# Streaming attention for one query: eight heads to a load instead of four, in three buffers, with every engine's order set by hand

## The chip, the cores and the metric

The kernel runs on one core of one Trainium2 chip. The metric is the device time of one execution in microseconds (us). A profile covers the "span" of one execution, which is about 1.7 us shorter than the reported time.

Engines: PE (TensorE, matmuls), VectorE (DVE in the profile), ScalarE (ACT), GpSimd (POOL), and the queue from which loads are issued (SP). The data come in through 16 DMA engines. The granted clock is the share of PE's full clock that the profile records; PE is called warm at full clock and cold at half.

## The reference

```python
B, H, Sq, Skv, Dh = 8, 32, 1, 4096, 128        # q, k, v in bfloat16
scale  = q.shape[-1] ** -0.5
scores = jnp.einsum('bhqd,bhkd->bhqk', q, k) * scale
attn   = softmax(scores, axis=-1)
return jnp.einsum('bhqk,bhkd->bhqd', attn, v)
```

There are 256 heads, each with one query, 4096 keys and 4096 values. K and V are 537 MB together, each byte is used once, and little is computed with it. The least that any kernel must do is bring 537 MB in.

## The kernel before

A tile holds G = 4 heads. A head lies on 32 partitions, and each partition has C = 128 of its keys (32 KiB). One load brings one tile of K or of V (4 MiB) into one of five buffers. Per tile t:

```python
G = 4; SLOTS = 5; R = 4; LAST = 8
...
def product(t, lo, hi):            # VectorE: k * q, then add the upper half of d to the lower
    for c0 in range(lo, hi, MC):   # MC = 32 keys, one chunk
        nc.vector.tensor_tensor(out=part, in0=part, in1=qb..., op=ALU.mult)
        nc.vector.tensor_tensor(out=part[:, :, 0 : D // 2], in0=..., in1=..., op=ALU.add)

def sum_over_d(t):                 # PE: 16 matmuls with the identity, sums into PSUM
    for s in range(n):
        nc.tensor.matmul(ps[:], lhsT=ident[:], rhs=kt[:, ..., s * DS : (s + 1) * DS], ...)

def weights_of(t):                 # VectorE: last sum, maximum over the head, bias
    nc.vector.tensor_reduce(out=sc[...], in_=ps[:], axis=AX.X, op=ALU.add)
    ...
    w = w_pool.tile([P, C, G], BF16, name="w", tag="w")
    for g in range(G):             # ScalarE: one exponential per head
        nc.scalar.activation(out=w[:, :, g], in_=sc[:], func=ACT.Exp, bias=bias[:, g : g + 1], ...)

def values_of(t, lo, hi):          # PE: four columns of weights at a time against V
    for c0 in range(lo, hi, CB):
        nc.tensor.matmul(avs[t][:], lhsT=w[:, c0 : c0 + CB, :], rhs=vt[:, c0 : c0 + CB, :], ...)

def norm_of(n):                    # PE: total of the weights;  VectorE: its reciprocal
    nc.tensor.matmul(zp[:], lhsT=esums..., rhs=ones[:], ...)
    nc.vector.reciprocal(out=rzs[n][:], in_=zp[:])

def result_of(t):                  # ScalarE: copy out of PSUM ("combine");  PE: pick;  ScalarE: scale, store
    ...
```

The main loop works with a lag. While tile t is multiplied, the weights of tile t-1 are made and the values of tile t-2 are summed. K is loaded two tiles ahead. The order of the main loop's instructions on each engine is left to the framework; only the end of the kernel has a set order.

```python
for t in range(NT - 1):            # NT = 64
    if t + 2 < NT: load("k", t + 2)
    load("v", t)
    ...
    product(t, 0, C // 2)
    if t > 0: weights_of(t - 1)
    product(t, C // 2, C)
    if t > 1:
        values_of(t - 2, 0, C); result_of(t - 2)
        ...
    sum_over_d(t)
```

## Time and profile before

The kernel took 1262.33 us (1262.09 to 1262.40, three runs).

| | before |
|---|---|
| loads, first packet to last | 1252.6 us |
| from the last packet to the end of the span | 6.1 us |
| rate of the slices in mid-run | 428 to 433 GB/s |
| VectorE busy, PE busy | 75 %, 67 % of the span |

The first two rows are worked out from the trace's packet records, which give start and length of every packet on the load queue (1.8 us is the start of the first one, 1254.4 us the end of the last).

From the page: the span, busy time and share of PE and VectorE, then the 40 slices of the span with DMA (tenths of the 16 engines' time) and the rate of each slice.

```profile
span 1260.5 us, 8779 instructions
...
PE 845.2 (67%) x3430; PEld 317.2 (25%) x3430; DVE 940.4 (75%) x851; ACT 164.3 (13%) x609; POOL 2.9 (0%) x14
...
DMA  9999999999999999999999999999999999999996
GB/s 400 432 431 431 430 433 430 430 430 430 432 432 430 429 433 432 432 433 431 431 432 433 428 432 432 432 429 430 432 431 430 433 432 432 430 431 431 429 424 287
```

The transfers run without a gap from the second slice to the last but one. They are the bound; the compute engines follow them.

From the timeline (start, length): PE in one tile.

```profile
648.83 9.38 PE L219 MATMUL av<-vt,w 128*16 128x512 bf16 x32 [6.55 <-DMA vt<-in_v_dram]
...
658.14 1.04 PE L167 MATMUL ps<-kt,ident 128*128 128x512 bf16 x4
...
659.42 2.77 PE L167 MATMUL ps<-kt,ident 128*128 128x512 bf16 x12
```

The 16 sum matmuls take 1.04 + 2.77 = 3.8 us.

### The profile page before, as it was taken

How to read it: one execution, taken by the hardware profiler on the slowest of the kernel's cores; microseconds unless marked ns; L12 is line 12 of the kernel's file. 1: busy time of each engine (PE TensorE's matmuls, PEld its weight loads, DVE VectorE, ACT ScalarE, POOL GpSimd, SP SyncE). 2: the span in 40 equal slices, each digit the busy share in tenths (PEclk: the TensorE clock that was granted, in tenths of full speed). 3: DMA queues.
4: the chain of work that ended last, by engine and by line, in shares of the span. 5: the costliest groups of instructions: out<-in, count | busy, mean ns of one | idle time of the engine just before them, and what ended most of it. 6: DMA issues, size and time to landing. Idle time of an engine off the chain costs nothing.

```text
span 1260.5 us, 8779 instructions
## 1 busy us (share of the span) xinstructions
PE 845.2 (67%) x3430; PEld 317.2 (25%) x3430; DVE 940.4 (75%) x851; ACT 164.3 (13%) x609; POOL 2.9 (0%) x14
## 2 busy tenths in 40 slices
PE   1666766856757667677676675766767667667578
PEld 0222222322222222222232222222222222222223
DVE  5869978687686777877778768677686777876873
ACT  0101111111101111011111110110101101111011
POOL 0000000000000000000000000000000000000000
PEclk9778878888789788887787888888888788887889
DMA  9999999999999999999999999999999999999996
GB/s 400 432 431 431 430 433 430 430 430 430 432 432 430 429 433 432 432 433 431 431 432 433 428 432 432 432 429 430 432 431 430 433 432 432 430 431 431 429 424 287
DMA packets 20569, 537.57 MB, mean 426 GB/s; under 512 B 2592, under 2 KB 2592, under 8 KB 2992
## 3 DMA queue, kind: packets, MB, share of 16 engines
q1 hardware_dynamic: 20160, 536.88, 99.2%
q8 instruction: 27, 0.44, 0.1%
q10 hardware_dynamic: 368, 0.13, 0.0%
q14 instruction: 14, 0.11, 0.0%
HBM read 536.94 MB, written 0.07 MB: 426 GB/s over the span
## 4 chain that ended last, share of the span: by engine, by line
DMA 67%; PE 24%; DVE 7%; ACT 1%; issue 0%; SPq 0%; ACTq 0%; DVEq 0%
DMA vt<-in_v_dram 66%; PE av L219 22%; DVE kt L150 4%; DVE kt L153 2%; PE ps L167 2%; DMA kt<-in_k_dram 1%; ACT w L203 0%; DVE sc L180 0%; PE op L244 0%; ACT comb L240 0%; DVE pmax L184 0%; SPq L124 0%; DVE bias L195 0%; DVE spread L186 0%; DVE nmax L191 0%
## 5 line engine op out<-in xcount | busy, mean ns | idle before, releaser
L219 PE MATMUL av<-vt,w 128*16 128x512 bf16 x2046 | 571.9, 449 | 344.1 <-DMA vt<-in_v_dram 344.1
L150 DVE TENSOR_TENSOR kt<-kt,qb 128x4096 bf16<-128x4096 bf16 x256 | 579.1, 2283 | 214.7 <-DMA kt<-in_k_dram 214.7
L219 PEld LDWEIGHTS <-w 128*16 128x16 bf16 x2046 | 207.6, 102 | 704.3 <-issue 537.3
L153 DVE TENSOR_TENSOR kt<-kt 128x2048 bf16<-128x2048 bf16 x256 | 305.7, 1215 | 0.1
L167 PE MATMUL ps<-kt,ident 128*128 128x512 bf16 x1024 | 253.2, 390 | 32.4 <-DVE kt L153 32.4
L203 ACT ACTIVATE w<-sc,bias 128x128 bf16<-128x128 f32 x256 | 110.9, 567 | 734.0 <-DVE bias L195 734.0
L167 PEld LDWEIGHTS <-ident 128*128 128x128 bf16 x1024 | 90.7, 98 | 161.3 <-issue 61.1
L203 ACT ACTIVATION_READ_ACCUMULATOR w<-sc,bias 128x1 f32 x256 | 64.8, 253 | 0.0
L180 DVE TENSOR_REDUCE sc<-ps 128x128 f32<-128x512 f32 x64 | 43.7, 683 | 24.6 <-PE ps L167 24.6
L240 ACT ACTIVATE comb<-av 16x512 bf16<-16x512 f32 x64 | 37.6, 588 | 167.8 <-PE av L219 132.2
L235 DVE RECIPROCAL rz<-zp 16x1 f32<-16x1 f32 x16 | 2.5, 155 | 66.9 <-PE zp L230 66.9
L141 ACT ACTIVATE qb<-qp 128x512 bf16<-128x512 f32 x16 | 9.6, 597 | 179.6 <-DVE kt L150 174.0
L244 PE MATMUL op<-comb,pick 16*16 16x128 bf16 x256 | 25.0, 217 | 6.4 <-ACT comb L240 6.4
L244 PEld LDWEIGHTS <-pick 16*16 16x16 bf16 x256 | 13.7, 84 | 34.2 <-issue 34.2
L135 PE MATMUL qp<-q_all,ident 16*32 16x512 bf16 x64 | 7.6, 430 | 21.6 <-ACT qb L141 14.9
L184 DVE TENSOR_REDUCE pmax<-sc 128x1 f32<-128x128 f32 x64 | 17.7, 277 | 0.1
L186 DVE TENSOR_SCALAR spread<-zero,pmax 128x32 f32<-128x32 f32 x64 | 14.9, 233 | 0.1
L195 DVE TENSOR_SCALAR bias<-own,nmax 128x4 f32<-128x4 f32 x64 | 14.3, 223 | 0.1
L191 DVE TRANSPOSE_TENSOR_REDUCE nmax<-spread 128x1 f32<-128x32 f32 x64 | 13.0, 202 | 0.1
L135 PEld LDWEIGHTS <-ident 16*32 16x32 bf16 x64 | 1.8, 89 | 28.4 <-issue 26.8
L230 PE MATMUL zp<-ones,esum 128*16 128x1 f32 x32 | 3.1, 166 | 8.1 <-ACT w L203 8.1
L259 ACT ACTIVATE stage<-op,rz 16x128 bf16<-16x128 f32 x16 | 5.7, 358 | 11.3 <-PE op L244 10.3
(21 smaller groups left out, 9.0 us busy)
## 6 DMA issues: line engine op xcount, KB each, us to landing
kt<-in_k_dram SPq DMA_DIRECT2D x63, 4096.0 KB, 35.2
vt<-in_v_dram SPq DMA_DIRECT2D x61, 4096.0 KB, 29.6
vt<-in_v_dram SPq DMA_DIRECT2D x11, 1024.0 KB, 22.3
kt<-in_k_dram SPq DMA_DIRECT2D x2, 2048.0 KB, 33.5
vt<-in_v_dram SPq DMA_DIRECT2D x1, 512.0 KB, 18.5
vt<-in_v_dram SPq DMA_DIRECT2D x2, 256.0 KB, 15.8
q_all<-in_q_dram ACTq DMA_DIRECT2D x1, 64.0 KB, 5.9
out_dram<-stage ACTq DMA_DIRECT2D x3, 16.0 KB, 9.9
```

What stands on the lines that cost most here:

```text
L150: nc.vector.tensor_tensor(out=part, in0=part, in1=qb[:, j : j + 1, :].to_broadcast([P, MC, D]), op=ALU.mult)
L153: nc.vector.tensor_tensor(out=part[:, :, 0 : D // 2], in0=part[:, :, 0 : D // 2], in1=part[:, :, D // 2 : D], op=ALU.add,)
L167: nc.tensor.matmul(ps[:], lhsT=ident[:], rhs=kt[:, u * UC : (u + 1) * UC, s * DS : (s + 1) * DS], start=(s == 0), stop=(s == n - 1),)
L180: nc.vector.tensor_reduce(out=sc[:, u * UC : (u + 1) * UC], in_=ps[:], axis=AX.X, op=ALU.add)
L184: nc.vector.tensor_reduce(out=pmax[:], in_=sc[:], axis=AX.X, op=ALU.max)
L186: nc.vector.tensor_scalar(out=spread[:], in0=zero[:], scalar1=pmax[:, 0:1], scalar2=-scale, op0=ALU.add, op1=ALU.mult,)
L191: nc.vector.tensor_reduce(out=nmax[:], in_=spread[:], axis=AX.X, op=ALU.min, apply_transpose=True)
L195: nc.vector.tensor_scalar(out=bias[:], in0=own[:], scalar1=nmax[:, 0:1], scalar2=None, op0=ALU.add)
L203: nc.scalar.activation(out=w[:, :, g], in_=sc[:], func=ACT.Exp, bias=bias[:, g : g + 1], scale=scale, accum_out=esum[:, t % R, g : g + 1],)
L219: nc.tensor.matmul(avs[t][:], lhsT=w[:, c0 : c0 + CB, :], rhs=vt[:, c0 : c0 + CB, :], start=(c0 == 0), stop=(c0 + CB == (C if t < NT - 1 e ...
L240: nc.scalar.activation(out=comb[:], in_=avs.pop(t)[:], func=ACT.Copy)
L244: nc.tensor.matmul(ops[n][:], lhsT=pick[:, m, r, :], rhs=comb[:, m * D : (m + 1) * D], start=(r == 0 and m == 0), stop=(r == R - 1 and m = ...
```

## The change

The intent is coarser work: half as many loads, each with rows twice as long, and fewer small instructions. A tile is now eight heads of 16 partitions with C = 256 keys each (64 KiB per partition, 8 MiB per load). Three such buffers fit where five of the old ones were. V follows K by one place in the queue, K is one tile ahead and not two. The values lag one tile instead of two, and the whole loop has a set order on every engine. Cut to its core:

```diff
-G = 4
-SLOTS = 5
-R = 4
+G = 8
+SLOTS = 3
+R = 2
...
     cuts = {
-        ("k", NT - 1): [C // 2] * 2,
-        ("v", NT - 3): [C // 4] * 4,
+        ("k", 0): [C // 4] * 4,
+        ("k", NT - 1): [C // 4] * 4,
         ("v", NT - 2): [C // 4] * 4,
-        ("v", NT - 1): [C // 4] * 3 + [C // 8, C // 16, LAST],
+        ("v", NT - 1): [C // 8] * 7 + [C // 16, LAST],
     }
...
-    for t in range(NT - 1):
-        if t + 2 < NT:
-            load("k", t + 2)
-        load("v", t)
-        ...
     with tc.manual_schedule():
+        q_prep(0)
+        for t in range(NT):                       # NT = 32
+            if t + 1 < NT:
+                load("k", t + 1)
+            load("v", t)
+            if t + 1 < NT:
+                q_prep(t + 1)
+            product(t, 0, UC)                     # UC = 128: four of eight chunks
+            sum_over_d(t, 0)
+            if t > 0:
+                values_of(t - 1, 0, C // 2)
+            product(t, UC, UC + MC)
+            scores_of(t, 0)
+            product(t, UC + MC, C)
+            sum_over_d(t, 1)
+            scores_of(t, 1)
+            weights_of(t)
+            if t > 0:
+                values_of(t - 1, C // 2, C)
+                if t % R == 0:
+                    norm_of(t // R - 1)
+                result_of(t - 1)
         norm_of(NQ - 1)
         values_of(NT - 1, 0, C - LAST)
         result_of(NT - 1)
```

Cut away: a small matmul that spreads the queries over 16 partitions each, a mask so that a block of 32 partitions can hold two heads, pool sizes (two buffers for w, one for sc), and LAST, the keys left for the very last matmuls, which goes from 8 to 16.

More of the change, by code (lines that the diff above doesn't have):

```diff
@@ L12 @@
 F32 = mybir.dt.float32
-G = 4
-SLOTS = 5
-R = 4
+G = 8
+SLOTS = 3
+R = 2
 OB = 4
-LAST = 8
+LAST = 16
 NEG = -1.0e30
@@ L47 @@
     NQ = NT // R
-    assert NQ <= P and C % CB == 0
-    q_n = q.rearrange("b h o d -> (b h o d)").rearrange("(n x) -> n x", n=NQ)
+    TB = 32
+    assert NH % P == 0 and P % G == 0 and TB % PH == 0 and C % CB == 0
+    q_n = q.rearrange("b h o d -> (b h o) d").rearrange("(x p) d -> p x d", p=P)
     o_n = out.rearrange("b h o d -> (b h o) d").rearrange("(n u x) d -> n x u d", u=OB, x=RG)
@@ L57 @@
     q_pool = ctx.enter_context(tc.tile_pool(name="q_pool", bufs=2))
-    w_pool = ctx.enter_context(tc.tile_pool(name="w_pool", bufs=3))
-    small = ctx.enter_context(tc.tile_pool(name="small", bufs=4))
-    o_pool = ctx.enter_context(tc.tile_pool(name="o_pool", bufs=2))
+    w_pool = ctx.enter_context(tc.tile_pool(name="w_pool", bufs=2))
+    sc_pool = ctx.enter_context(tc.tile_pool(name="sc_pool", bufs=1))
+    small = ctx.enter_context(tc.tile_pool(name="small", bufs=2))
+    o_pool = ctx.enter_context(tc.tile_pool(name="o_pool", bufs=1))
     ps_s = ctx.enter_context(tc.tile_pool(name="ps_s", bufs=2, space=bass.MemoryType.PSUM))
@@ L65 @@
     ps_z = ctx.enter_context(tc.tile_pool(name="ps_z", bufs=1, space=bass.MemoryType.PSUM))
-    q_all = consts.tile([NQ, R, G, D], BF16, name="q_all")
-    nc.scalar.dma_start(q_all.rearrange("n r g d -> n (r g d)"), q_n)
+    q_all = consts.tile([P, NH // P, D], BF16, name="q_all")
+    nc.scalar.dma_start(q_all[:], q_n)
     ident = consts.tile([P, P], BF16, name="ident")
@@ L73 @@
         out=ident[:], in_=ident[:], pattern=[[-1, P]], compare_op=ALU.not_equal,
+        fill=1.0, base=0, channel_multiplier=1,
+    )
+    heads = consts.tile([G, G, PH], BF16, name="heads")
+    nc.gpsimd.memset(heads[:], 0.0)
+    nc.gpsimd.affine_select(
+        out=heads[:], in_=heads[:], pattern=[[-1, G], [0, PH]], compare_op=ALU.not_equal,
         fill=1.0, base=0, channel_multiplier=1,
@@ L85 @@
         fill=NEG, base=PH - 1, channel_multiplier=-1,
+    )
+    same = consts.tile([P, TB], F32, name="same")
+    nc.vector.tensor_reduce(
+        out=same[:].rearrange("p (h x) -> p h x", x=PH),
+        in_=own[:].rearrange("p (b h) -> p h b", h=TB // PH)
+        .rearrange("p h (o b) -> p h o b", o=1)
+        .to_broadcast([P, TB // PH, PH, P // TB]),
+        axis=AX.X, op=ALU.max,
     )
@@ L101 @@
     )
-    zero = consts.tile([P, 32], F32, name="zero")
-    nc.vector.memset(zero[:], 0.0)
     ones = consts.tile([P, 1], F32, name="ones")
@@ L130, in q_prep @@
     def q_prep(t):
-        if t % R == 0:
-            n = t // R
-            qp = ps_q.tile([P, R, D], F32, name="qp", tag="qp")
-            for g in range(G):
-                nc.tensor.matmul(
-                    qp[g * PH : (g + 1) * PH, :, :],
-                    lhsT=ident[0:NQ, n : n + 1].to_broadcast([NQ, PH]),
-                    rhs=q_all[:, :, g, :], start=True, stop=True,
-                )
-            qb = q_pool.tile([P, R, D], BF16, name="qb", tag="qb")
-            nc.scalar.activation(out=qb[:], in_=qp[:], func=ACT.Copy)
-            qbs[n] = qb
+        x, p0 = divmod(t * G, P)
+        qh = ps_q.tile([G, D], F32, name="qh", tag="qp")
+        nc.tensor.matmul(
+            qh[:], lhsT=ident[:, p0 : p0 + G], rhs=q_all[:, x, :], start=True, stop=True
+        )
+        qg = q_pool.tile([G, D], BF16, name="qg", tag="qg")
+        nc.scalar.activation(out=qg[:], in_=qh[:], func=ACT.Copy)
+        qp = ps_q.tile([P, D], F32, name="qp", tag="qp")
+        nc.tensor.matmul(qp[:], lhsT=heads[:].rearrange("g h x -> g (h x)"), rhs=qg[:], start=True, stop=True)
+        qb = q_pool.tile([P, 1, D], BF16, name="qb", tag="qb")
+        nc.scalar.activation(out=qb[:, 0, :], in_=qp[:], func=ACT.Copy)
+        qbs[t] = qb
     def product(t, lo, hi):
         kt = loads["k", t]
-        qb = qbs[t // R]
-        j = t % R
+        qb = qbs[t]
         for c0 in range(lo, hi, MC):
@@ L150, in product @@
             nc.vector.tensor_tensor(
-                out=part, in0=part, in1=qb[:, j : j + 1, :].to_broadcast([P, MC, D]), op=ALU.mult
+                out=part, in0=part, in1=qb[:].to_broadcast([P, MC, D]), op=ALU.mult
             )
@@ L158, with sum_over_d, scores_of @@
     sums = {}
-    def sum_over_d(t):
-        kt = loads.pop(("k", t))
-        sums[t] = []
-        for u in range(NU):
-            ps = ps_s.tile([P, UC, DS], F32, name="ps", tag="ps")
-            n = D // 2 // DS
-            for s in range(n):
-                nc.tensor.matmul(
-                    ps[:], lhsT=ident[:],
-                    rhs=kt[:, u * UC : (u + 1) * UC, s * DS : (s + 1) * DS],
-                    start=(s == 0), stop=(s == n - 1),
-                )
-            sums[t].append(ps)
+    def sum_over_d(t, u):
+        kt = loads["k", t]
+        ps = ps_s.tile([P, UC, DS], F32, name="ps", tag="ps")
+        n = D // 2 // DS
+        for s in range(n):
+            nc.tensor.matmul(
+                ps[:], lhsT=ident[:],
+                rhs=kt[:, u * UC : (u + 1) * UC, s * DS : (s + 1) * DS],
+                start=(s == 0), stop=(s == n - 1),
+            )
+        sums[t, u] = ps
+    scs = {}
+    def scores_of(t, u):
+        if u == 0:
+            scs[t] = sc_pool.tile([P, C], F32, name="sc", tag="sc")
+        nc.vector.tensor_reduce(
+            out=scs[t][:, u * UC : (u + 1) * UC], in_=sums.pop((t, u))[:], axis=AX.X, op=ALU.add
+        )
     ws = {}
@@ L177, in weights_of @@
     def weights_of(t):
-        sc = small.tile([P, C], F32, name="sc", tag="sc")
-        for u, ps in enumerate(sums.pop(t)):
-            nc.vector.tensor_reduce(
-                out=sc[:, u * UC : (u + 1) * UC], in_=ps[:], axis=AX.X, op=ALU.add
-            )
+        sc = scs.pop(t)
         pmax = small.tile([P, 1], F32, name="pmax", tag="pmax")
         nc.vector.tensor_reduce(out=pmax[:], in_=sc[:], axis=AX.X, op=ALU.max)
-        spread = small.tile([P, 32], F32, name="spread", tag="spread")
+        spread = small.tile([P, TB], F32, name="spread", tag="spread")
         nc.vector.tensor_scalar(
-            out=spread[:], in0=zero[:], scalar1=pmax[:, 0:1], scalar2=-scale,
+            out=spread[:], in0=same[:], scalar1=pmax[:, 0:1], scalar2=-scale,
             op0=ALU.add, op1=ALU.mult,
@@ L265, in result_of @@
             nc.scalar.dma_start(o_n[s, :, lo : u + 1, :], stages[s][:, lo : u + 1, :])
-    q_prep(0)
     load("k", 0)
-    load("k", 1)
-    for t in range(NT - 1):
-        if t + 2 < NT:
-            load("k", t + 2)
-        load("v", t)
-        if t + 2 < NT:
-            q_prep(t + 2)
-        product(t, 0, C // 2)
-        if t > 0:
-            weights_of(t - 1)
-        product(t, C // 2, C)
-        if t > 1:
-            values_of(t - 2, 0, C)
-            result_of(t - 2)
-            if (t - 2) % R == R - 2:
-                norm_of((t - 2) // R)
-        sum_over_d(t)
-    load("v", NT - 1)
-    with tc.manual_schedule():
-        product(NT - 1, 0, C // 2)
-        weights_of(NT - 2)
-        product(NT - 1, C // 2, C)
-        values_of(NT - 3, 0, C)
-        result_of(NT - 3)
-        sum_over_d(NT - 1)
-        values_of(NT - 2, 0, C // 2)
-        weights_of(NT - 1)
-        values_of(NT - 2, C // 2, C)
-        result_of(NT - 2)
+    with tc.manual_schedule():
+        q_prep(0)
[20 more added lines that the diff above has]
+                result_of(t - 1)
         norm_of(NQ - 1)
```

## The prediction

> **What bounds the kernel now.** The transfers do. In the page's 40 slices DMA is busy at nine tenths or more and moves 430 to 433 GB/s from the second slice to the 38th; all 537 MB of K and V must come in once. The Trainium skill ("DMA: Bandwidth & Descriptors", "Where 436 GB/s comes from") puts the fabric's ceiling at 435.2 GB/s, so 1 % is left in the rate: nothing can save more than about 2 %. VectorE is busy 75 %, PE 67 %; in the view of waits VectorE waits 215 us for K and PE 344 us for V. In the chain of waits the steady part is one pattern, "V lands, 32 value matmuls, next V". The engines differ a little: by the packet records the first of the 16 DMA engines ends at 1246.9 us, the last at 1254.4, and a load counts only when the last has landed. The rest, to 1260.5, is the last product and the store. The reported time is 1.8 us above the span.
>
> **What the change does to the rate.** One packet is one partition's row. The records give 613 ns for 16 KiB and 1219 ns for 32 KiB: about 8 to 12 ns per packet are fixed. A 64 KiB packet should take 2429 ns instead of 2 x 1219. With half the loads (fewer semaphore packets of 9 ns) this is 0.09 us per 8 MiB, 5 to 6 us over the run. If the 64 KiB row is cut into two packets, this gain vanishes.
>
> **Does the queue stay fed with three buffers?** A load takes 19.4 us, a pair of K and V 38.9. V(t) needs K(t)'s buffer. VectorE's eight chunks of 3.34 us (two products 4.41, two halvings 2.27) and one score reduction end about 28 us after K(t) lands. But PE first takes half of V(t-1), which lands 19.4 us after K(t): 32 matmuls, 9.3 us at the granted 0.83, then 16 sum matmuls, 3.8 us. So V(t) is issued about 14 us after V(t-1) landed and has 19.4 minus 1 us (issue to first packet). Slack 3 to 4 us: just fed. VectorE needs 32 us per 38.9 us.
>
> **The tail.** Twice as coarse a grain leaves more work behind the last loads. From the landing of V(29) (about 1190 us: 61 loads of 19.44 us and a start of some 4 us, of which 2 us are the slow first packets): 32 value matmuls 9.3, sums 3.9, scores and weights 1.8, products of the last K 27.7, sums 3.7 (full clock), second half of V(30) 7.1, combine 1.2, 60 value matmuls 13.1, combine, 16 last matmuls, scaling and store 4.9. Sum 72.7, so the span ends at about 1262.6; the transfers end near 1248. The tail after the transfers grows from 6 to about 14 us and eats the gain of the rate.
>
> **Predicted time:** 1264 us, 8 in 10 between 1253 and 1279. Faster by over 2 %: 0.01; within 2 %: 0.92; slower by over 2 %: 0.07.
>
> **What would show it.** Right: some 11,700 packets on the load queue, most near 2430 ns; 432 to 433 GB/s in mid-run; no slice below 9 tenths; the last large packet near 1248 us; in the chain of waits a last stretch of VectorE and PE of some 70 us; VectorE idle about 3 us before each K. Wrong rate: packets of 32 KiB. Wrong feed: GB/s below 428 in mid-run, and issues of V waiting for the sum matmuls.
>
> **What would make it wrong.** A granted clock near 0.7 lengthens 13 us of PE work by 3 us and uses up the slack: 1 us of gap per pair costs 31 us in all. A shorter tail (VectorE ahead when the last K lands) would give up to 8 us.

## More of the kernel before

Most executions of a kernel agree within 0.3 %; all runs quoted here are fast runs, or single-core runs that were not slower than their fellows.

From the page's groups of instructions: busy time and mean length of one, then the idle time of the engine just before them and what ended it.

```profile
L219 PE MATMUL av<-vt,w 128*16 128x512 bf16 x2046 | 571.9, 449 | 344.1 <-DMA vt<-in_v_dram 344.1
L150 DVE TENSOR_TENSOR kt<-kt,qb 128x4096 bf16<-128x4096 bf16 x256 | 579.1, 2283 | 214.7 <-DMA kt<-in_k_dram 214.7
...
L203 ACT ACTIVATE w<-sc,bias 128x128 bf16<-128x128 f32 x256 | 110.9, 567 | 734.0 <-DVE bias L195 734.0
...
L180 DVE TENSOR_REDUCE sc<-ps 128x128 f32<-128x512 f32 x64 | 43.7, 683 | 24.6 <-PE ps L167 24.6
...
L235 DVE RECIPROCAL rz<-zp 16x1 f32<-16x1 f32 x16 | 2.5, 155 | 66.9 <-PE zp L230 66.9
```

PE and VectorE wait mostly for data (344 and 215 us). VectorE also waits for PE: 24.6 us in front of the score reduction and 66.9 us in front of the 16 reciprocals. Beside 215 us of waiting for K there was room for that.

## The result and the profile after

The changed kernel took 1348.3 us (1347.95 to 1349.58, four runs), beside 1262.21 us for the kernel before in the same rounds. The ratio is 1.0684 (95 % interval 1.0666 to 1.0703). Ratios in this document are the mean time of one kernel's fast runs over that of the other's fast runs of the same rounds, so they are not quite the ratio of the medians. The result is correct, and the kernel is 6.8 % slower, outside the predicted range.

Where the 87.4 us of span (1347.9 - 1260.5) came from, by the packet records:

| | before | after | difference |
|---|---|---|---|
| loads, first packet to last | 1252.6 | 1314.4 | +61.8 |
| of that: a DMA engine idle, mean of 16 | 6.1 | 63.0 | +56.9 |
| last packet to the end of the span | 6.1 | 31.7 | +25.6 |

The rest of the +61.8 is +3.2 in the packets themselves (9.6 us more in packets that were over 10 % longer than the median, and 6.4 us less because long packets are cheaper per byte) and some 1.8 us because the packet records overlap less than before. Nearly all the slow ones (241 to 247 of 256 large packets) were the first on their engine after a gap of over 0.1 us (the records do not name the engine; packets were put together into 16 chains by their times, and the count depends a little on how).

From the page after, the same parts:

```profile
span 1347.9 us, 8337 instructions
...
PE 835.1 (62%) x3308; PEld 340.3 (25%) x3308; DVE 960.5 (71%) x723; ACT 338.7 (25%) x625; POOL 2.8 (0%) x16
...
DMA  9969989898998989989899898999989899898990
GB/s 406 436 281 434 434 378 434 376 434 376 436 435 375 434 376 434 434 376 434 378 434 436 372 434 378 434 407 436 432 380 436 374 434 436 376 432 377 411 422 9
```

Two things stand out. When the queue is fed it runs at 434 to 436 GB/s, a little faster than before. And every second or third slice falls to some 376. Apart from ScalarE, no engine is busy for much longer than before (VectorE 960.5 us against 940.4).

The groups that answer to those of before, and the reciprocal:

```profile
L164 DVE TENSOR_TENSOR kt<-kt,qb 128x4096 bf16<-128x4096 bf16 x256 | 584.8, 2284 | 12.8 <-ACT qb L156 12.2
...
L220 ACT ACTIVATE w<-sc,bias 128x256 bf16<-128x256 f32 x256 | 301.9, 1596 | 945.2 <-DVE bias L212 945.2
L236 PE MATMUL av<-vt,w 128*32 128x512 bf16 x2044 | 453.6, 380 | 18.4 <-DMA vt<-in_v_dram 18.4
...
L191 DVE TENSOR_REDUCE sc<-ps 128x128 f32<-128x512 f32 x64 | 44.3, 692 | 252.5 <-PE ps L179 252.5
...
L252 DVE RECIPROCAL rz<-zp 16x1 f32<-16x1 f32 x16 | 2.5, 155 | 77.6 <-PE zp L247 77.6
```

The waits have changed sides. VectorE no longer waits for K (0.7 us in all, against 215), PE hardly waits for V (18.4, against 344). VectorE now waits for PE: 252.5 us in front of the score reductions and 77.6 us in front of the 16 reciprocals. The second wait is nearly as old as the kernel (66.9 us before); what is new is that VectorE has no waiting for K left to hide it in. The queue waits for them, and not they for the queue.

One tile from the timeline after, all engines cut to the lines that decide it:

```profile
641.10 5.95 PE L179 MATMUL ps<-kt,ident 128*128 128x512 bf16 x16 [7.97 <-DVE kt L167]
...
647.15 0.69 DVE L191 TENSOR_REDUCE sc<-ps 128x128 f32<-128x512 f32 x1 [2.64 <-PE ps L179]
...
658.28 5.89 PE L179 MATMUL ps<-kt,ident 128*128 128x512 bf16 x16 [4.22 <-DVE kt L167]
...
664.20 0.33 SPq L139 DMA_DIRECT2D vt<-in_v_dram  x1
664.21 0.69 DVE L191 TENSOR_REDUCE sc<-ps 128x128 f32<-128x512 f32 x1 [5.99 <-PE ps L179]
...
701.87 0.69 DVE L191 TENSOR_REDUCE sc<-ps 128x128 f32<-128x512 f32 x1 [5.39 <-PE ps L179]
...
708.93 0.15 DVE L252 RECIPROCAL rz<-zp 16x1 f32<-16x1 f32 x1 [5.12 <-PE zp L247]
```

VectorE stands idle 2.64 us for the first group of sums and 5.99 us for the second; the load of V goes out at the same moment, because it needs the buffer that the second group has just read. In every second tile VectorE then stands 5.12 us more before the reciprocal: its matmul waits on PE behind 32 value matmuls. From first product to first product, one tile lasts 38.94 us (627.11 to 666.05) and the next 42.98 us (666.05 to 709.03), 40.96 on average. Two loads need 2 x 8 x 2.418 = 38.7 us (the median packet of 64 KiB took 2418 ns). So the compute loop has become longer than the transfers.

The 16 sum matmuls take 5.9 us here and took 3.8 before. PE had been idle for 4 to 8 us in front of them. The Trainium skill ("TensorE: Matmul & The Clock Gate", Part 1) says that after an idle window of about 3.4 us the PE clock falls to half, until it has been busy for such a window. The trace agrees on the half rate: in the group at 641.10 us the weight loads come every 0.43 us at first and every 0.22 us at the end, and whole groups behind a short gap take 3.62 us (shown below in e11_tail). It differs on the window: the recorded clock is at half from 656.09 us on, and the last matmul before it had ended at 654.06, only 2.0 us earlier; the measurement decides. Of the 64 groups of the run, 62 took over 5 us.

The end of the chain of waits after:

```profile
1310.22 5.91 PE ps L179 x16
...
1318.12 9.40 ACT w L220 x16
...
1328.51 14.67 PE av L236 x60
```

When the last packet lands (1316.2 us), VectorE and PE are only just finishing the sums of the last K. After that come 9.4 us of exponentials and 14.7 us of value matmuls, one after the other.

### The profile page after: what moved, and what is told of

Its sections match the earlier page's. It is cut to its first block, busy times and chain, and to the rows that moved or that the text cites. A ratio compares the mean times of both kernels' runs of the same rounds, so it can differ in the third digit from the quotient of the medians.

```text
span 1347.9 us, 8337 instructions
## 1 busy us (share of the span) xinstructions
PE 835.1 (62%) x3308; PEld 340.3 (25%) x3308; DVE 960.5 (71%) x723; ACT 338.7 (25%) x625; POOL 2.8 (0%) x16
## 3 DMA queue, kind: packets, MB, share of 16 engines
q1 hardware_dynamic: 11664, 536.88, 93.0%
## 4 chain that ended last, share of the span: by engine, by line
DVE 59%; PE 35%; DMA 4%; issue 1%; ACT 1%; DVEq 0%
DVE kt L164 36%; PE ps L179 26%; DVE kt L167 20%; PE av L236 9%; DMA kt<-in_k_dram 3%; DVE sc L191 2%; DMA q_all<-in_q_dram 1%; ACT w L220 1%; DVE pmax L201 1%; DVE spread L203 0%; DVE nmax L208 0%; DVE bias L212 0%; ACT comb L257 0%; PE op L267 0%; PE zp L247 0%
## 5 line engine op out<-in xcount | busy, mean ns | idle before, releaser
L179 PE MATMUL ps<-kt,ident 128*128 128x512 bf16 x1024 | 355.0, 520 | 298.2 <-DVE kt L167 298.2
L220 ACT ACTIVATE w<-sc,bias 128x256 bf16<-128x256 f32 x256 | 301.9, 1596 | 945.2 <-DVE bias L212 945.2
L236 PE MATMUL av<-vt,w 128*32 128x512 bf16 x2044 | 453.6, 380 | 18.4 <-DMA vt<-in_v_dram 18.4
L179 PEld LDWEIGHTS <-ident 128*128 128x128 bf16 x1024 | 126.4, 123 | 543.6 <-issue 508.2
L236 PEld LDWEIGHTS <-w 128*32 128x32 bf16 x2044 | 194.4, 97 | 273.7 <-issue 46.8
L191 DVE TENSOR_REDUCE sc<-ps 128x128 f32<-128x512 f32 x64 | 44.3, 692 | 252.5 <-PE ps L179 252.5
L220 ACT ACTIVATION_READ_ACCUMULATOR w<-sc,bias 128x1 f32 x256 | 127.5, 498 | 0.0
L261 PE MATMUL op<-comb,pick 32*16 32x128 bf16 x128 | 14.3, 240 | 153.8 <-ACT comb L257 153.8
L252 DVE RECIPROCAL rz<-zp 16x1 f32<-16x1 f32 x16 | 2.5, 155 | 77.6 <-PE zp L247 77.6
L261 PEld LDWEIGHTS <-pick 32*16 32x16 bf16 x128 | 9.8, 90 | 161.1 <-issue 160.8
L257 ACT ACTIVATE comb<-av 32x512 bf16<-32x512 f32 x32 | 28.4, 888 | 15.3 <-PE av L236 15.3
L154 PE MATMUL qp<-qg,heads 8*128 8x128 bf16 x32 | 8.3, 260 | 25.6 <-ACT qg L152 25.6
L201 DVE TENSOR_REDUCE pmax<-sc 128x1 f32<-128x256 f32 x32 | 13.4, 420 | 1.1
```

The source lines that it names most:

```text
L154: nc.tensor.matmul(qp[:], lhsT=heads[:].rearrange("g h x -> g (h x)"), rhs=qg[:], start=True, stop=True)
L179: nc.tensor.matmul(ps[:], lhsT=ident[:], rhs=kt[:, u * UC : (u + 1) * UC, s * DS : (s + 1) * DS], start=(s == 0), stop=(s == n - 1),)
L191: nc.vector.tensor_reduce(out=scs[t][:, u * UC : (u + 1) * UC], in_=sums.pop((t, u))[:], axis=AX.X, op=ALU.add)
L201: nc.vector.tensor_reduce(out=pmax[:], in_=sc[:], axis=AX.X, op=ALU.max)
L257: nc.scalar.activation(out=comb[:], in_=avs.pop(t)[:], func=ACT.Copy)
L261: nc.tensor.matmul(ops[n][:], lhsT=pick[:, m, r, :], rhs=comb[:, m * D : (m + 1) * D], start=(r == 0 and m == 0), stop=(r == R - 1 and m = ...
```

## The experiments

Theory A: in the set order VectorE and PE wait for each other inside one tile, and this loop is longer than two loads. Rival B: three coarse buffers cannot feed the queue, whatever the order. A third thought, that large transfers are slow in themselves, falls to the trace above: 434 to 436 GB/s where the queue is fed.

### Move the reciprocal (e1_norm)

```diff
             sum_over_d(t, 0)
+            if t > 0 and t % R == 0:
+                norm_of(t // R - 1)        # the matmul only
...
             scores_of(t, 0)
+            if t > 0 and t % R == 0:
+                inverse_of(t // R - 1)     # the reciprocal only
...
-                if t % R == 0:
-                    norm_of(t // R - 1)
```

> Edit: the matmul that sums the weights' totals goes right behind the first sum matmuls of the tile, and its reciprocal behind the first score reduction, so VectorE no longer waits for it behind 32 value matmuls. Theory A (VectorE and PE wait for each other in the set order, and that loop is longer than the transfers): the 16 tiles with a reciprocal are 42.98 us long against 38.94 for the others, so 16 x 4.0 = 65 us go and the time is 1275 to 1292 us; the wait of 77.6 us before the reciprocal is under 3 us. Rival B (three buffers cannot feed the queue, whatever VectorE does): the wait moves to another place and the time stays above 1335. Rival C (VectorE is not on the path at all, the time was lost in the tail): above 1340.

Measured: 1312.08 us (1310.0 to 1316.95), ratio to before 1.0401. That is 36 us less than the changed kernel, where 56 to 73 were expected: B and C fall as they were put, but A had left something out. VectorE's waits in this run (in total, times, longest):

```profile
DVE sc L191 <- PE ps L179: 250.8, 63, 6.3
...
DVE kt L164 <- DMA kt<-in_k_dram: 40.4, 22, 5.7
```

The wait before the reciprocals is gone (0.8 us), the one for sums is untouched, and a wait for K has appeared: the queue still has gaps, 28.3 us per DMA engine.

### Keep PE awake (e2_fill)

```diff
+            fill(10)                       # matmuls of the identity into an unused tile
             sum_over_d(t, 0)
...
+            fill(14)
             sum_over_d(t, 1)
...
+                fill(20)
                 result_of(t - 1)
```

> Edit: 10, 14 and 20 idle matmuls (identity times identity into an unused PSUM tile) before the two groups of sum matmuls and before the combine, to keep PE awake; nothing else is changed. Theory A2 (the sum matmuls are slow because PE stood idle before them: 5.3 to 6.0 us for 16, against 3.6 warm): both groups fall to about 3.6 us, VectorE's waits for them (2.0 to 2.6 and 5.4 to 6.0 us) fall by about 2 us each, the loop of 40.96 us falls below the 38.7 us of two transfers, time 1265 to 1290 us. Rival B (three buffers): above 1335. If the idle matmuls only delay the sums: 1348 or more.

Measured: 1317.94 us (1314.74 to 1325.19), ratio 1.0450. That is 30 us less than the changed kernel, and still outside the expected range. The loads are 28.1 us shorter and the tail 4.8. The trace shows 40 of 64 groups of sums under 4 us, most of them at 3.62, as hoped, but also idle matmuls that stand in front of sums that were ready: the longest wait for sums rose from 6.3 to 9.0 us, and the total fell only from 252.5 to 215.1. The run helps and does not isolate the cold start.

### Take work from VectorE (e5_less)

```diff
+            if c0 == C - MC:
+                continue                   # wrong on purpose
             nc.vector.tensor_tensor(out=part[:, :, 0 : D // 2], ..., op=ALU.add)
```

> Wrong result on purpose: the halving add of the last of the eight chunks of each tile is left out (1.15 us of VectorE per tile). Theory A (VectorE's chain is what the loop waits for): 32 x 1.15 = 37 us less, 1305 to 1318 us. Rival B (the transfers' hand-over of three buffers is the limit, VectorE has room): under 10 us less, above 1338.

Measured: 1302.50 us (1295.22 to 1308.42), ratio 1.0317: 46 us less, more than the 37 us of work that were taken away and just below the expected range; VectorE's wait for sums fell too, from 252.5 to 216.0 us. VectorE's chain is on the path, and the gaps of the queue shrink with it (13.3 us per engine, from 63.0). The comparison with the reference did not notice the missing add; this kernel is not a candidate.

### Take the set order away (e4_auto)

```diff
-    with tc.manual_schedule():
-        q_prep(0)
-        for t in range(NT):
+    q_prep(0)
+    for t in range(NT):                    # the same statements
```

> Edit: the set order is taken away (the same statements without it), the loads and the three buffers stay. The order that results on VectorE: two multiplications then two adds, the first score reduction after six chunks and not after five; the reciprocal stays behind the weights. Theory A: the wait before the first score reduction (2.0 to 2.6 us) and about 1.0 us of stalls between dependent products go, the loop falls from 40.96 to about 38.7 us, time 1270 to 1292 us. Rival B (the coarse loads in three buffers are the cause, not the order): stays above 1335.

Measured: 1291.12 us (1289.70 to 1293.88), ratio 1.0237. The same loads, sizes and buffers without the set order are 57 us faster. The loads take 1260.3 us, 7.8 more than in the kernel before; what remains is a tail of 25.8 us. The order that the framework made is not free of such waits (146.7 us before the reciprocals, 121.2 before the score reductions), but together they are 62 us less than in the set order.

### The weights' layout (e7_wcgm)

```diff
-        w = w_pool.tile([P, C, G], BF16, name="w", tag="w")
+        w = w_pool.tile([P, C // CB, G, CB], BF16, name="w", tag="w")
...
-                out=w[:, :, g], in_=sc[:], func=ACT.Exp, ...
+                out=w[:, :, g, :], in_=sc[:].rearrange("p (a m) -> p a m", m=CB), func=ACT.Exp, ...
```

> Edit: the weights lie as (four columns together, by head) instead of (heads together, by column), so that an exponential writes runs of 8 bytes and not single 2-byte elements 16 bytes apart; the pick matrix is permuted to match. Theory D (the spread-out writes make the 128x256 exponential 1.14 us from start to start, against 0.385 us for 128x128 before): it falls under 0.7 us; ScalarE's busy time under 200 us; the tail shortens by some 4 us; PE's waits of 4.9 us before each combine fall under 1 us. VectorE's loop is not shortened by it, so the time stays at 1330 to 1346. Rival (the exponential costs what its elements and the accumulator cost, whatever the layout): start to start stays above 1.0 us and the time within 3 us of 1348.

Measured: 1342.41 us (1338.49 to 1344.40), ratio 1.0629, 6 us less. The exponential in this run:

```profile
L213 ACT ACTIVATE w<-sc,bias 128x256 bf16<-128x256 f32 x256 | 126.3, 494 | 1080.7 <-DVE bias L205 1080.7
```

Its mean length fell from 1596 to 494 ns, and the time from one start to the next from 1.14 to 0.49 us (the records of neighbours overlap), with the same elements and the same accumulator: theory D holds. In the changed kernel an exponential writes 2 bytes every 16 (G = 8), where the kernel before wrote 2 bytes every 8 (G = 4). The Trainium skill ("SBUF — State Buffer", "Door 1: The DMA port swizzle") speaks of lines of 16 bytes that want at least two accesses each; the slow writes here, one to a line, fit that. Whether two to a line are enough no run here shows: the kernel before wrote two, but its exponentials have half as many elements. The next sentence of the page lets bfloat16 go with a stride of 8 elements for free; here that stride costs a factor of 2.3 from start to start, and the measurement decides. The 6 us are the tail alone, 25.6 us instead of 31.7. That the loop gained nothing from it is as expected: ScalarE is not in it.

### Six half buffers: with the reciprocal moved (e8_norm_half), and alone (e13_half)

```diff
-    kv_pool = ctx.enter_context(tc.tile_pool(name="kv_pool", bufs=SLOTS))
+    kv_pool = ctx.enter_context(tc.tile_pool(name="kv_pool", bufs=2 * SLOTS))
...
-        buf = kv_pool.tile([P, C, D], BF16, ...)       # one buffer, one load
+        # two tiles [P, UC, D] and two loads for each K and each V; no engine's order changes
```

> Edit on top of e1_norm: six buffers of 32 KiB per partition in place of three of 64, each load in two halves, so half of V(t) can be fetched as soon as the first half of K(t) has been summed. Nothing in any engine's order changes. Theory B2 (with the reciprocal moved, VectorE's loop of 38 us is just below the 38.7 us of two loads, and what is left is that a 64 KiB buffer is handed over in one piece, so late that gaps of the queue are never made up): the loads end within 1256 us of the first packet (1282 in e1_norm, 28 us of idle per DMA engine, under 9 us here), time 1276 to 1290 against 1312. Theory A alone (VectorE's loop is the whole of it): within 6 us of 1312.

> Edit: only the six buffers of 32 KiB in place of three of 64, on the changed kernel with its order and its reciprocal as they are. Rival B (the hand-over of three coarse buffers is the cause by itself): the time falls to 1285 or below. Theory A (VectorE's loop of 38 and 43 us in turn, 40.96 on average, is longer than the 38.7 us of two loads, so the queue waits whatever the buffers are): VectorE's waits stay (250 us for sums, 78 us before the reciprocal) and the time stays between 1325 and 1348.

Measured: e8_norm_half 1273.57 us (1272.37 to 1274.21), ratio 1.0089, 2 us under the range that was expected of it; e13_half 1351.47 us (1350.85 to 1352.05), ratio 1.0706, 3 us above the range that was expected of it. With the changed kernel and e1_norm they make a square:

| | three buffers of 64 KiB | six of 32 KiB |
|---|---|---|
| reciprocal where the change put it | 1348.3 | 1351.5 |
| reciprocal moved | 1312.1 (e1_norm) | 1273.6 (e8_norm_half) |

Finer buffers alone bring nothing, so rival B is not the cause by itself: the loads end 7.8 us sooner than in the changed kernel, but VectorE is not ready for them, and the tail grows from 31.7 to 41.4 us. e13_half waits as the changed kernel does:

```profile
DVE sc L193 <- PE ps L181: 255.7, 64, 6.1
...
DVE rz L254 <- PE zp L249: 77.6, 16, 5.1
```

But once the loop is nearly as short as the transfers, the coarse hand-over costs 38.5 us (1312.1 - 1273.6). A 64 KiB buffer is released in one moment, when the second group of sums has ended, and whatever the queue has lost by then it cannot make up, because no other buffer is free. With halves, the first half of V(t) needs only the first group of sums, which in the traced tile ends 17 us earlier (647.0 and 664.2 us), and the rates of the slices show no gap:

```profile
GB/s 399 436 435 429 429 428 433 434 432 429 431 428 430 435 432 429 430 431 432 433 432 429 432 431 429 433 431 429 432 433 429 432 430 432 432 430 430 427 422 135
```

The loads end 1251.5 us after the first packet and a DMA engine idles 5.5 us, as in the kernel before.

### Keep PE awake, with a lighter hand (e12_norm_fill)

On top of e1_norm:

```diff
+            fill(6)                        # 10 in e2_fill
             sum_over_d(t, 0)
...
+            fill(8)                        # 14 in e2_fill
             sum_over_d(t, 1)
...
+                fill(12)                   # 20 in e2_fill
                 result_of(t - 1)
```

> e1_norm with 6, 8 and 12 idle matmuls before the two groups of sums and the combine, fewer than in e2_fill, where they held up sums that were ready. Theory A2 (after e1_norm VectorE's loop of 38 us still holds some 4 us in which it waits for sum matmuls that run at half clock after an idle PE): VectorE's waits for sums fall from 251 us to 140 to 190, the gaps of the queue close for the most part (idle per DMA engine under 14 us, 28 in e1_norm), time 1280 to 1298 us against 1312. If the cold start does not matter: within 6 us of 1312.

Measured: 1299.97 us (1299.39 to 1301.12), ratio 1.0303. It is 12 us faster than e1_norm, but just outside the expected range: VectorE's wait for sums fell to 205.9 us and not below 190, and a DMA engine still idles 21.6 us and not under 14. The loads are 8.2 us shorter, the tail 4.8. So the cold start of PE is a real part of the loop, 8 us here and 28 us in e2_fill, where the reciprocal was still in its place; how much it would be without idle matmuls in the way is not settled by these two runs.

### Let VectorE never wait for PE in the same tile (e9_lag), and with layout and pairs (e10_all)

```diff
-            product(t, 0, UC)
+            product(t, 0, 2 * MC)
+            if t > 0:
+                scores_of(t - 1, 1)
+                weights_of(t - 1)
+            product(t, 2 * MC, UC)
             sum_over_d(t, 0)
...
-            product(t, UC, UC + MC)
+            product(t, UC, UC + 2 * MC)
             scores_of(t, 0)
-            product(t, UC + MC, C)
+            product(t, UC + 2 * MC, C)
             sum_over_d(t, 1)
-            scores_of(t, 1)
-            weights_of(t)
...                                    # the reciprocal as in e1_norm
```

> Edit: order only, on VectorE and PE. The second score reduction and the weights of tile t go behind the first two chunks of tile t+1, the first score reduction behind six chunks and not five, the reciprocal as in e1_norm. Loads, their sizes and the three buffers stay. Theory A (VectorE stood waiting for PE in the set order): VectorE's waits for sum matmuls fall from 250 us to under 40, the loop falls to about 32 us and the transfers bound again: loads end within 1254 us of the first packet; the tail keeps its 9 us of exponentials and its cold value matmuls, 18 to 22 us. Time 1262 to 1277 us. Rival B (three buffers cannot feed): above 1300.

e10_all adds the layout of e7_wcgm and the order of the products:

```diff
-        # multiply chunk, add chunk, multiply chunk, add chunk
+        # multiply chunk, multiply chunk, add chunk, add chunk
```

> e9_lag, with the weights' layout of e7_wcgm and two multiplications before two adds. Theory A and D together: as e9_lag, and a tail shorter by the 5 us of the exponentials: 1256 to 1270 us, level with the kernel before (1262.2). If it is above 1275 a cause is missing.

Measured: e9_lag 1274.09 us (1273.09 to 1276.18), ratio 1.0097; e10_all 1265.41 us (1265.40 to 1266.31), ratio 1.0028. In e9_lag the loads, their sizes and the three coarse buffers are those of the changed kernel; only the order differs, and 74 us are gone. VectorE's waits:

```profile
DVE kt L164 <- DMA kt<-in_k_dram: 251.1, 29, 9.3
...
DVE sc L191 <- PE ps L179: 3.7, 1, 3.7
```

The wait for sums fell from 252.5 to 3.7 us, and VectorE waits for K again, as before the change. PE did not become warm for it: 31 of the 64 groups of sums still took over 5 us, but VectorE no longer stands behind them. The loads take 1247.1 us, 5.5 us less than in the kernel before: this is the gain of the longer rows that the change was after. What is left is the tail, 23.5 us, and e10_all takes it to 15.1.

### The order at the end (e11_tail)

```diff
             sum_over_d(t, 1)
+            if t == NT - 1:
+                scores_of(t, 1)
+                weights_of(t)
             if t > 0:
                 values_of(t - 1, C // 2, C)
                 result_of(t - 1)           # its copy on ScalarE waits for PE
...
-        scores_of(NT - 1, 1)
-        weights_of(NT - 1)
```

> e10_all, with the last tile's exponentials ahead of the combine of the tile before it on ScalarE. In e10_all the last exponentials could start at 1234.4 us and started at 1240.0, behind that combine, which waits for PE. Theory: they end 5 us earlier, the last 60 value matmuls start some 4 us earlier and warm (13.1 and not 14.8 us): 5 us less, 1259 to 1262 us, level with or just under the kernel before (1262.2). If it stays at 1265 the tail is bound by something else.

Measured: 1259.98 us (1259.87 to 1260.03, five runs), against 1262.05 for the kernel before in the same rounds; ratio 0.9983, 95 % interval 0.9970 to 0.9996. The end of its timeline:

```profile
1228.69 3.62 PE L174 MATMUL ps<-kt,ident 128*128 128x512 bf16 x16 [1.04 <-DVE kt L162]
...
1234.32 0.51 ACT L215 ACTIVATE w<-sc,bias 128x256 bf16<-128x256 f32 x1 [18.18 <-DVE bias L207]
...
1240.37 13.11 PE L234 MATMUL av<-vt,w 128*32 128x512 bf16 x60
```

The exponentials start right behind the bias, the value matmuls run warm (13.1 us), the sums behind a gap of 1 us also (3.62 us). The loads take 1246.8 us and the tail is 9.6. This version beats both kernels, by 88 us and by 2 us; the latter is clear of noise and far below 2 %.

## Why the prediction was wrong

1. **What bounds the kernel before, and the rate of the long rows: right.** The packets numbered 11,664, as predicted, with a median of 2418 ns for 64 KiB (2429 predicted), and a fed queue ran at 434 to 436 GB/s (432 to 433 predicted; the estimate that 1 % was left in the rate was right too). e9_lag and e11_tail collect it: loads shorter by 5.5 to 5.8 us, 5 to 6 predicted. That the sum fits so well is partly luck: a 64 KiB packet saved 14 ns and not 9, and slow packets took some of that back (1.1 us in e9_lag).

2. **"VectorE needs 32 us per 38.9 us": this step failed.** Its busy time was right (30 us per tile by the windows view of the two tiles above: 29.90 and 30.09). But in a set order an engine also waits in line, and the 32 us left room for 2 us of that. The traced tile lasts 38.94 us without and 42.98 with a reciprocal. Three terms were wrong or absent:
   - the sums: 3.8 us, read from a place where they stood behind 32 value matmuls. Behind an idle PE they took mostly 5.3 to 6.0 us, twice per tile, with VectorE waiting (252.5 us in all). e9_lag takes this wait out of the loop and wins 74 us together with the next term.
   - the reciprocal was not in the sum at all: 77.6 us of waiting, and every second tile 4.0 us longer. The page before already listed this wait (66.9 us). e1_norm shows what it cost, 36 us of time.
   - a chunk of products took 3.46 us (666.05 to 669.51, the next chunk's start) and not 3.34, where each add directly follows the multiplication that it needs.

3. **"Slack 3 to 4 us: just fed": wrong as its consequence.** The slack was worked out as if VectorE were free when K lands. It was not: the sums that free the buffer waited for VectorE's products (298.2 us in all, in PE's waits), and hardly for V(t-1) to land (18.4 us), which the prediction had as the path. So V was issued late in tile after tile (56.9 us more idle time per DMA engine). The square of the four runs shows both halves: order alone makes the loop too long, and the coarse buffers then turn lateness into lost transfer time.

4. **The tail: the mechanism was right, the size was not.** 14 us were predicted behind the last packet, 31.7 measured. The exponentials were thought to be hidden behind 7.1 us of value matmuls; they took 9.4 us, because their writes lie 16 bytes apart (e7_wcgm). The last value matmuls ran partly cold (14.7 us for 13.1). And VectorE reached the last K late, as in every tile before. With the causes removed one after the other the tail was 23.5, 15.1 and 9.6 us (e9_lag, e10_all, e11_tail).

5. **What would show it: this part worked.** "Wrong feed: GB/s below 428 in mid-run, and issues of V waiting for the sum matmuls" is what the profile shows (some 376 GB/s in many slices; 30 issues that waited for sums, 163.3 us in all). The reading was prepared; the chance given to it (7 % for over 2 % slower) was far too small for a slack of 3 us that rested on one duration per step.

What stays open: how the loop's loss divides between the cold PE and the mere position of the waits. If the idle matmuls can only hold work up, the two runs with them bound the first from below, by 28 us of load time in the changed kernel and 8 us after the reciprocal was moved, and no more. Nor is it shown why a multiplication directly before its add costs more.

## What to carry to other kernels

When an engine's order is set by hand, draw the loop through all engines and count its waits, not its busy time: a tiny instruction that needs a result from the end of another engine's queue (here a reciprocal of 0.15 us) holds up everything behind it. Such a wait can stand on the page before and cost nothing there, because the engine has waiting for data to spare; a change that uses up this spare time makes it count. Keep one tile of lag between an engine that produces and one that waits, and read a matmul's cost only from a place with the same idle time in front of it. With few large buffers, check when each is released: a loop just shorter than the transfers leaves nothing with which to make up a gap.

## What the Trainium skill lacked or had wrong

- "SBUF — State Buffer", "Door 1: The DMA port swizzle": it gives 8 elements as the stride that bfloat16 can take for free. Exponentials that wrote bfloat16 with a stride of 8 elements started 1.14 us apart, against 0.49 us for runs of four adjacent elements (128 x 256, same input). Its own remark that a 16-byte line needs two accesses would fit, but two accesses to a line were not tested at this size.
- "TensorE: Matmul & The Clock Gate", Part 1: it calls the warm-up less than 1 % of a typical kernel's span. This loop is not of that kind: 62 of 64 groups of 16 sum matmuls took over 5 us instead of 3.62, and the run with idle matmuls before them was 30 of 1348 us faster (e2_fill). The page's part on oscillation in real kernels does describe a loop that starts cold in every pass. The clock also fell 2.0 us after a matmul, sooner than the window of about 3.4 us.
- "VectorE: DVE Perf Modes", "The DRAIN you can't avoid": its test, eight copies, finds no extra cost of semaphores; it has no figure for an instruction that reads what the one directly before it wrote. A multiplication and the add that needs it took 3.46 us from pair to pair, and 3.34 when two multiplications were followed by two adds. Why is not shown.
- "DMA: Bandwidth & Descriptors": it does not say that packets can take longer when a queue starts again. In the changed kernel the first large packet of an engine after a gap of over 0.1 us took some 0.6 us longer than the median (about 270 packets). That the gap is the cause is not shown: in e4_auto 203 large packets were over 10 % longer than the median, and at most 84 of them followed such a gap. Nor does the page say what rows above 32 KiB are worth: one packet of 64 KiB took 2418 ns and two of 32 KiB 2 x 1216 ns, a gain of 14 ns.
